# Row sums of an attention kernel: two accumulators, one addition per unit, and a moved row-sum matmul

## The chip, the cores and the metric

The kernel runs on 1 core of one Trainium2 chip. The core has a matrix engine (TensorE, PE in the profile, with PEld for its weight loads), a vector engine (VectorE, DVE), a scalar engine (ScalarE, ACT), GpSimd (POOL) and SyncE (SP), whose queue issues nearly all DMAs here. The metric is the device time of one execution in microseconds.

## The reference

Four layers in turn on x of 2048 x 1024: attention, spectral filter, attention, spectral filter, each with a layer norm ahead and a residual behind. Only the attention's core is touched by the timing questions here.

```python
def _A_ref(x, wqkv, wo):            # B, S, D = 1, 2048, 1024; H = 32 heads of 32
    qkv = (x @ wqkv).reshape(B, S, 3, H, Dh).transpose(2, 0, 3, 1, 4)
    q, k, v = qkv[0], qkv[1], qkv[2]
    scores = jnp.einsum("bhqd,bhkd->bhqk", q, k) * (Dh ** -0.5)
    p = _softmax(scores, axis=-1)
    o = jnp.einsum("bhqk,bhkd->bhqd", p, v)
    return o.transpose(0, 2, 1, 3).reshape(B, S, D) @ wo

def _B_ref(x, w_r, w_i):
    X = rfft2(x) * (w_r + 1j * w_i)
    return irfft2(X, s=(S, D))

x = x + _A_ref(_layernorm(x), A_wqkv, A_wo)
x = x + _B_ref(_layernorm(x), B_w_r, B_w_i)
# and both once more, with the same weights
```

## The kernel before

The softmax is computed without a maximum per row: a bound per group of heads, from norms of q and k, is subtracted (`norms`, `mkbias`), the exponentials are summed, and the product with V is divided by the sum at the end.

**Stages of a layer.** A prologue (`ln`, L300 to L324) normalises 16 tiles of 128 rows, splits each into a high and a low float16 half (`split`, L165: ScalarE makes the high half at L167, VectorE the low half at L168) and transposes both by DMA (L322, on the SP queue). Beside it the first projections run. Then comes the chunk loop, then the end of the output projection with the folding for the spectral stage, then `spectral`.

**The chunk loop** (from L626) runs over 8 groups of 4 heads, in each over 4 chunks `c` of 512 queries, and in each over 16 units `kt` of 128 keys, so a layer has 512 units and 32 chunks. A unit does this:

- `S` (L552): 12 matmuls give the scores of 4 heads into two PSUM tiles of 128 x 2 x 512 (L558), and ScalarE takes the exponential of each into a tile `p` of 128 x 1024 (L562). The pool `psS` has 3 such PSUM tiles, and `pp` has 8 tiles `p`, that is 4 units.
- `PV` (L564): every second unit, the products with V for the two units before it (L568).
- `add` (L575): VectorE adds the unit's two tiles `p` to the two accumulators `acc[0]` and `acc[1]`, 128 x 1024 each (L581). Unit 0 has no addition; unit 1 writes `p0 + p1` into the accumulator (L579).
- a fill in odd units: 8 to 24 matmuls of the next groups' projections (`qk_chunk`, L340; `v_tiles`, L384), or of the output projection in the last two groups (`wo_part`, `wo_rest`, L443). `qk_chunk` collects a sum in the one PSUM bank of `psX`, which is free again when L167 and L168 have read it.

`fin` (L583) ends a chunk: four matmuls with a matrix of ones sum the accumulators over the partitions (L587, into a tile of `psS`), VectorE transposes (L588), takes the reciprocal (L590), transposes back (L593) and scales the output (L594). `out` (L597) splits it to float16 at unit 5 of the next chunk (L600 on ScalarE, L601 on GpSimd) and stores it.

`add` of a unit is written two units later. So the last unit of a chunk is added in the text of unit 1 of the next chunk, and `fin` stands right behind it, after the scores of unit 1 and ahead of that unit's fill.

**What sets the order.** In the chunk loop TensorE and ScalarE run in the order in which the program writes their instructions (`manual_schedule`). The order on VectorE, GpSimd and SP, and everywhere outside the loop but for TensorE at the end of the attention, is chosen by a planner that places an instruction when it expects its inputs. Each engine then works through its queue in order. Slots of a pool are waited for tile by tile: a tile's slot is free when all that used the tile is done.

**Where the accumulators lie.** A buffer `R` of 128 x 16384 floats holds x, K, Q, V and, in its last 2048 columns, the two accumulators (L204, L205). The profile calls all of them `R`.

`pp` serves other stages too: the normalised tile and its two halves (`xn` and `hl`, L316 to L318), residual tiles (`xres`), folding tiles (L512), and tiles `tt` and `sd` in `spectral` (L966, L984).

Of the kernel before, what the change touches and what calls it, by code (L numbers as in the profile page):

```python
# [188 lines left out]
class AttnPools:  # L189


    def __init__(self, tc):
        self.tc = tc
        self.low = Pools(tc, "left")
        self.big = self.low("at_x", 1).tile([128, 16384], F32, name="big")
        self.right = Pools(tc, "right")
        r = self.right("at_r", 1).tile([128, 16384], F32, name="R")
        self.x = r.rearrange("p (t d) -> p t d", d=1024)
        k = r.bitcast(F16).rearrange("p (t a n) -> p t a n", a=2, n=2048)
        self.k = [k[:, i] for i in (3, 4, 5)]  # L200
        self.q = k[:, 2]
        v = r.rearrange("p (a t c) -> p a t c", t=16, c=128)
        self.v = [v[:, i] for i in (0, 1, 6)]
        a = r.rearrange("p (a j n) -> p a j n", j=2, n=512)  # L204
        self.acc = [a[:, i] for i in (14, 15)]  # L205

    def close(self):
        self.small.close()
        self.right.close()
        self.low.close()  # L210

    def open_small(self):
        small = self.small = Pools(self.tc, "left")
        self.pp = small("at_p", 8)
        self.qp = small("at_q", 1)
        self.oc = small("at_oc", 1)
        self.sgp = small("at_stage", 3)
        self.wqp = small("at_wqk", 2)
        self.wvp = small("at_wv", 1)
        self.sq = small("at_sq", 1)  # L220
        self.on = small("at_on", 2)
        self.on2 = small("at_on2", 2)
        self.sm = small("at_sm", 2)
        self.stages = [(self.sgp, "wst")] * 3 + [(self.on, "zt")] * 2 + [(self.on2, "ohl")] * 2
# [45 lines left out]
def attention(nc, tc, layer, ap, xin, yd, wts, wo, cst, dram, flags):  # L270
# [3 lines left out]

    W, prep = wts.W, wts.prep
    od = dram.tile([2, NG, 128, 2048], F16, name=f"od{layer}")
    small, psum = ap.small, Pools(tc, None)
# [22 lines left out]
    def ln(t0, n):  # L300
# [13 lines left out]
        for i in range(n):  # L314
            t = t0 + i
            xn = pp.tile([128, 1024], F32, name="xn", tag="p")  # L316
            nc.scalar.activation(xn, ap.x[:, t], AF.Identity, bias=b[:, i:i + 1], scale=r[:, i:i + 1])
            hl = pp.tile([128, 2, 1024], F16, name="hl", tag="p")  # L318
            split(nc, hl[:, 0], hl[:, 1], xn, SX)
# [126 lines left out]
    def xres(c, t):  # L446
        if c == 3:
            x = pp.tile([128, 1024], F32, name="xres", tag="p")
        else:
# [58 lines left out]
    def fold_rests():  # L508

        r, b = scale_bias(mvs, 12, 1.0)  # L510
        for t in SPILL + [t for t in range(12) if t not in SPILL]:
            f = pp.tile([128, 1024], F32, name="xn", tag="p")  # L512
            nc.scalar.activation(f, wo_dst[t], AF.Identity, bias=b[:, t:t + 1], scale=r[:, t:t + 1])
# [35 lines left out]

    P, O, acc = {}, {}, ap.acc  # L550

    def S(g, c, kt):  # L552

        s = [psS.tile([128, 2, 512], F32, name="s") for _ in range(2)]
        for i, (a, b) in enumerate(((0, 0), (0, 1), (1, 0))):
            for h in range(4):
                r = slice(32 * h, 32 * h + 32)
                nc.tensor.matmul(s[h // 2][:, h % 2], K[g][r, a, kt * 128:kt * 128 + 128],  # L558
                                 Q[g][r, b, c * 512:c * 512 + 512], start=i == 0, stop=i == 2)
        for hf in range(2):  # L560
            p = P[g, c, kt, hf] = pp.tile([128, 2, 512], F32, name="p")
            nc.scalar.activation(p, s[hf], AF.Exp, bias=bias[g], scale=SCALE / (SQ * SQ))  # L562

    def PV(g, c, kt):  # L564
        if kt == 0:
            O[g, c] = psO.tile([128, 512], F32, name="o")
        for h in range(4):
            nc.tensor.matmul(O[g, c][32 * h:32 * h + 32], V[g][:, kt, 32 * h:32 * h + 32], P[g, c, kt, h // 2][:, h % 2],  # L568
                             start=kt == 0, stop=kt == NKT - 1)
# [5 lines left out]
    def add(g, c, kt):  # L575
        for hf in range(2):
            p = P[g, c, kt, hf]
            if kt == 1:
                nc.vector.scalar_tensor_tensor(acc[hf], P[g, c, 0, hf], 1e-34, p, op0=ALU.add, op1=ALU.add)  # L579
            elif kt:  # L580
                nc.vector.tensor_add(acc[hf], acc[hf], p)  # L581

    def fin(g, c):  # L583
        zt = on.tile([128, 16, 32], F32, name="zt")
        z = psS.tile([128, 2, 512], F32, name="s")[:, 0]
        for h in range(4):
            nc.tensor.matmul(z[32 * h:32 * h + 32], cst["ones"], acc[h // 2][:, h % 2], start=True, stop=True)  # L587
        nc.vector.transpose(zt.rearrange("p a b -> p (a b)"), z)  # L588
# [17 lines left out]

    pend, done, late = [], [], []
    fill, lwo, wof = filler(), load_wo(), wo_parts()
# [16 lines left out]
    with tc.manual_schedule(engines={mybir.EngineType.PE, mybir.EngineType.Activation}):  # L625
        for g in range(NG):  # L626
# [3 lines left out]
            for u in range(NCH * NKT):  # L630
                c, kt = divmod(u, NKT)
                S(g, c, kt)
                if kt % 2 == 0:
                    for w in pend:
                        PV(*w)
                    late = pend
                    pend = []
                for w in late[:1]:
                    add(*w)
                    if w[2] == NKT - 1:  # L640
                        fin(*w[:2])
                        done = [w[:2]]
                late = late[1:]
# [106 lines left out]
def spectral(nc, tc, ap, yd, xout, a, cst, fast, flags=None, nxt=None):  # L750
# [209 lines left out]
    nc.sync.dma_start(mi, a["mm" + sfx][:, 2:4])  # L960

    def t2(i, g):
        pt = ps.tile([128, 4, 128], F32, name="ps")
        for j in range(4):
            nc.tensor.transpose(pt[:, j], bufA[:, g, :, 4 * i + j], ident)
        tt = ap.pp.tile([128, 4, 128], F32, name="tt", tag="p")  # L966
        nc.scalar.copy(tt, pt)
        return tt

    sd = {}  # L970

    def ai(i, tt):
# [9 lines left out]
        if i < 14:  # L982
            if i % 2 == 0:
                sd[0] = ap.pp.tile([128, 8, 128], F32, name="sd", tag="p")  # L984
            e = ap.on.tile([128, 4, 128], F32, name="e", tag="zt")
# [251 lines left out]
```

## Time and profile before

| | |
|---|---|
| median of 3 runs | 3907.49 us (3906.37 to 3912.81) |
| profiled execution, span from first to last instruction | 3906.3 us; the page gives no time outside it |
| mean granted TensorE clock | 0.986 |
| chunk loop, layer 0 / layer 1 | from about 126 to 1660 us / 2081 to 3600 us |
| exponentials L562 | 2048 of 1.11 us |
| additions L581, L579 | 1792 and 128 |
| row-sum matmuls L587 | 64 groups of 4, recorded as 8 each |

A page gives the busy time of each engine and its share of the span, then groups of instructions in the form "line engine operation out<-in xcount | busy us, mean ns of one | idle us before them <-what ended it". Rows of the timeline give start, duration, engine, line, operation and count, and in brackets the idle time of the engine just before and what ended it. Rows of the chain give start, duration and what ran. SPq is the SP queue's own issue time. A view by line also lists who waited for that line, with microseconds and times. Matmul ends are modelled, and a float32 matmul shows as two records.

### The profile page before, as it was taken

The numbers are of one execution on the slowest core, as the hardware profiler recorded it, in microseconds if no ns is written. First come the engines' busy times: TensorE is split into PE (matmuls) and PEld (weight loads), VectorE is DVE, ScalarE is ACT, GpSimd is POOL, SyncE is SP. The second block draws the span as 40 slices with busy tenths as digits, with TensorE's granted clock in tenths as the row PEclk, the third lists the DMA queues.
The fourth block names the chain that finished last, engine by engine and source line by source line (L and its number), as shares of the span: only waits on it lengthen the run. The fifth ranks groups of instructions, "written<-read, shape, count | busy, mean of one in ns | idle before, by whom it ended". The sixth has DMA issues, their size and how long they took to land.

```text
span 3906.3 us, 79627 instructions
## 1 busy us (share of the span) xinstructions
PE 3737.0 (96%) x32951; PEld 1642.5 (42%) x32951; DVE 3181.5 (81%) x3793; ACT 2899.6 (74%) x3567; POOL 637.5 (16%) x560
## 2 busy tenths in 40 slices
PE   6999999999999999989989999999999999999998
PEld 4322432342234233368853334333423432333788
DVE  6689899889998987966665998889899888788554
ACT  4577787888788865657855888888888887666686
POOL 1111011101110200014321221122121102000143
PEclk9999999999999999999999999999999999999999
DMA  8000000000000221134170000000000002111333
GB/s 203 15 12 23 12 12 17 18 12 17 15 23 7 71 71 64 64 139 142 62 176 12 15 23 12 12 18 22 10 18 12 23 12 90 52 68 66 146 97 105
DMA packets 165573, 194.07 MB, mean 50 GB/s; under 512 B 74960, under 2 KB 120656, under 8 KB 164176
## 3 DMA queue, kind: packets, MB, share of 16 engines
q1 hardware_dynamic: 164912, 188.82, 15.2%
q8 instruction: 260, 4.26, 0.4%
q14 instruction: 113, 0.93, 0.1%
q10 hardware_dynamic: 288, 0.07, 0.0%
HBM read 123.83 MB, written 48.23 MB: 44 GB/s over the span
## 4 chain that ended last, share of the span: by engine, by line
PE 75%; DVE 10%; issue 7%; ACT 4%; DMA 2%; POOL 2%; SPq 0%; DVEq 0%; ACTq 0%; POOLq 0%
PE o L568 21%; PE s L558 17%; PE x L340 13%; PE x L384 7%; PE x L443 6%; ACT p L562 2%; DVE R L581 2%; PE ps L862 2%; PE ps L800 1%; PE s L587 1%; DMA w<-in_w 1%; PE ps L791 1%; PE s L443 1%; PE ps L977 1%; PE o L384 1%
## 5 line engine op out<-in xcount | busy, mean ns | idle before, releaser
L562 ACT ACTIVATE p<-s,bias 128x1024 f32<-128x1024 f32 x2048 | 2169.0, 1111 | 589.9 <-PE s L558 578.4
L581 DVE TENSOR_TENSOR R<-R,p 128x1024 f32<-128x1024 f32 x1792 | 2146.8, 1251 | 148.3 <-ACT p L562 144.2
L568 PE MATMUL o<-p,R 128*32 128x512 f32 x8192 | 986.1, 599 | 0.0
L340 PE MATMUL x<-big,wqk 128*128 128x512 f16 x2880 | 685.6, 384 | 21.9 <-DVE R L168 8.1
L558 PEld LDWEIGHTS <-R 32*128 32x128 f16 x12288 | 232.5, 92 | 780.2 <-issue 664.6
L340 PEld LDWEIGHTS <-wqk 128*128 128x128 f16 x3072 | 277.9, 98 | 460.1 <-issue 167.5
L558 PE MATMUL s<-R 32*128 32x512 f16 x6144 | 432.5, 379 | 19.1 <-ACT p L562 15.6
L558 PE MATMUL s<-Q,R 32*128 32x512 f16 x6144 | 433.0, 378 | 11.9 <-ACT p L562 10.6
L568 PEld LDWEIGHTS o<-p,R 128*32 128x32 f32 x8192 | 213.9, 109 | 525.6 <-issue 525.0
L601 POOL TENSOR_TENSOR ohl<-zt,ohl 128x512 f16<-128x512 f32 x62 | 180.3, 2907 | 1473.6 <-ACT ohl L600 1473.6
L384 PEld LDWEIGHTS <-big 128*128 128x128 f16 x3072 | 295.0, 99 | 159.7 <-issue 79.1
L384 PE MATMUL x<-wv,big 128*128 128x256 f16 x2688 | 323.2, 277 | 40.6 <-DMA big<-hl 34.6
L579 DVE SCALAR_TENSOR_TENSOR R<-p 128x1024 f32<-128x1024 f32 x128 | 153.9, 1204 | 198.7 <-ACT p L562 198.4
L344 POOL TENSOR_TENSOR sq<-R 128x512 bf16<-128x512 f16 x96 | 144.5, 1505 | 693.8 <-ACT R L167 690.6
L443 PE MATMUL x<-big 128*128 128x512 f16 x1050 | 237.4, 380 | 0.0
L443 PEld LDWEIGHTS <-big 128*128 128x128 f16 x1344 | 126.3, 98 | 177.3 <-issue 33.9
L910 DVE TENSOR_TENSOR H<-G,H 128x512 f16<-128x512 f32 (+1 forms) x68 | 46.9, 690 | 104.7 <-ACT H L909 104.6
L862 PE MATMUL ps<-cbi,H 128*128 128x256 f16 (+1 forms) x792 | 99.2, 273 | 5.6 <-ACT H L909 3.3
L855 ACT COPY U<-ps 64x256 f32<-64x256 f32 (+1 forms) x272 | 97.0, 357 | 8.5 <-PE ps L862 3.3
L855 ACT COPY B<-ps 64x256 f32<-64x256 f32 (+1 forms) x272 | 97.0, 356 | 6.7 <-PE ps L862 3.2
L344 POOL TENSOR_TENSOR sq<-Q 128x512 bf16<-128x512 f16 x32 | 44.6, 1395 | 319.7 <-ACT Q L167 319.7
L862 PE MATMUL ps<-cb,big 128*128 128x256 f16 x780 | 96.4, 273 | 0.0
(429 smaller groups left out, 3017.1 us busy)
## 6 DMA issues: line engine op xcount, KB each, us to landing
wst<-in_wp SPq DMA_DIRECT2D x96, 256.0 KB, 3.0
R<-y SPq DMA_DIRECT2D x32, 512.0 KB, 5.4
w<-in_w SPq DMA_DIRECT2D x60, 256.0 KB, 2.6
od<-ohl SPq DMA_DIRECT2D x56, 256.0 KB, 2.4
big<-od SPq DMA_DIRECT2D x16, 896.0 KB, 6.6
y<-R SPq DMA_DIRECT2D x20, 512.0 KB, 2.7
R<-in_x SPq DMA_DIRECT2D x16, 512.0 KB, 5.6
wst<-in_wo SPq DMA_DIRECT2D x32, 256.0 KB, 2.9
```

What stands on the lines that cost most here:

```text
L340: nc.tensor.matmul(ps, a, b, start=d == 0 and i == 0, stop=d == 7 and i == 2)
L344: nc.gpsimd.tensor_tensor(nrm[ph][:, c], t[:, 0], t[:, 0], op=ALU.mult)
L384: nc.tensor.matmul(ps[:, j], l, r, start=d == 0 and i == 0, stop=d == 7 and i == 2)
L443: nc.tensor.matmul(p, a, b, start=start and d == ds[0] and i == 0, stop=stop and d == ds[-1] and i == 2)
L558: nc.tensor.matmul(s[h // 2][:, h % 2], K[g][r, a, kt * 128:kt * 128 + 128], Q[g][r, b, c * 512:c * 512 + 512], start=i == 0, stop=i == 2)
L562: nc.scalar.activation(p, s[hf], AF.Exp, bias=bias[g], scale=SCALE / (SQ * SQ))
L568: nc.tensor.matmul(O[g, c][32 * h:32 * h + 32], V[g][:, kt, 32 * h:32 * h + 32], P[g, c, kt, h // 2][:, h % 2], start=kt == 0, stop=kt == ...
L579: nc.vector.scalar_tensor_tensor(acc[hf], P[g, c, 0, hf], 1e-34, p, op0=ALU.add, op1=ALU.add)
L581: nc.vector.tensor_add(acc[hf], acc[hf], p)
L601: eng.tensor_tensor(t[:, 1], r, t[:, 0], op=ALU.subtract)
L855: nc.scalar.copy(ov[64 * r:64 * r + 64, a0:a0 + m, x], tl[64 * x:64 * x + 64, :m, r])
L862: nc.tensor.matmul(out, l, r, start=k == 0, stop=k == len(mm_) - 1)
```

## The change

There are six edits.

1. `acc` becomes two accumulators of 128 x 2048: the old place in `R`, and a new pool `at_acc` of 8 KB per partition. Chunks use them in turn (`acc[c % 2]`).
2. The two exponentials of a unit go into the halves of one tile `p` of 128 x 4 x 512. `pp` has 4 tiles of double size instead of 8, and one addition of 128 x 2048 replaces two of 128 x 1024.
3. `fin` is called at unit 2 of the next chunk, right after `PV` of its units 0 and 1, and no longer at unit 1. `out` stays at unit 5.
4. `xn` and `hl` of the prologue share one double tile.
5. Residual and folding tiles and `sd` are halves of a double tile, handed out in turn by a new function `half`; the `tt` tiles of two steps share one.
6. The scratch for dynamic DMAs is set to 4096 bytes per partition.

```diff
-        a = r.rearrange("p (a j n) -> p a j n", j=2, n=512)
-        self.acc = [a[:, i] for i in (14, 15)]
+        self.acc0 = r[:, 14336:16384]
...
+    def half(self, name):
+
+        if self.halves % 2 == 0:
+            self.pair = self.pp.tile([128, 2, 1024], F32, name=name, tag="p")
+        self.halves += 1
+        return self.pair[:, (self.halves - 1) % 2]
+
     def open_small(self):
+        self.halves = 0
         small = self.small = Pools(self.tc, "left")
-        self.pp = small("at_p", 8)
+        self.pp = small("at_p", 4)
+        self.accp = small("at_acc", 1)
...
-            xn = pp.tile([128, 1024], F32, name="xn", tag="p")
+            pair = pp.tile([128, 2, 1024], F32, name="xn", tag="p")
+            xn, hl = pair[:, 0], pair[:, 1].bitcast(F16).rearrange("p (a n) -> p a n", a=2)
             nc.scalar.activation(xn, ap.x[:, t], AF.Identity, bias=b[:, i:i + 1], scale=r[:, i:i + 1])
-            hl = pp.tile([128, 2, 1024], F16, name="hl", tag="p")
...
-            x = pp.tile([128, 1024], F32, name="xres", tag="p")
+            x = ap.half("xres")
...
-            f = pp.tile([128, 1024], F32, name="xn", tag="p")
+            f = ap.half("xn")
...
-    P, O, acc = {}, {}, ap.acc
+    P, O, acc = {}, {}, [ap.acc0, ap.accp.tile([128, 2048], F32, name="acc")]
...
+        p = P[g, c, kt] = pp.tile([128, 4, 512], F32, name="p")
         for hf in range(2):
-            p = P[g, c, kt, hf] = pp.tile([128, 2, 512], F32, name="p")
-            nc.scalar.activation(p, s[hf], AF.Exp, bias=bias[g], scale=SCALE / (SQ * SQ))
+            nc.scalar.activation(p[:, 2 * hf:2 * hf + 2], s[hf], AF.Exp, bias=bias[g], scale=SCALE / (SQ * SQ))
...
     def add(g, c, kt):
-        for hf in range(2):
-            p = P[g, c, kt, hf]
-            if kt == 1:
-                nc.vector.scalar_tensor_tensor(acc[hf], P[g, c, 0, hf], 1e-34, p, op0=ALU.add, op1=ALU.add)
-            elif kt:
-                nc.vector.tensor_add(acc[hf], acc[hf], p)
+        t, p, q = acc[c % 2], *(P[g, c, k].rearrange("p h n -> p (h n)") for k in (kt, 0))
+        if kt == 1:
+            nc.vector.scalar_tensor_tensor(t, q, 1e-34, p, op0=ALU.add, op1=ALU.add)
+        elif kt:
+            nc.vector.tensor_add(t, t, p)
...
-            nc.tensor.matmul(z[32 * h:32 * h + 32], cst["ones"], acc[h // 2][:, h % 2], start=True, stop=True)
+            nc.tensor.matmul(z[32 * h:32 * h + 32], cst["ones"], acc[c % 2][:, 512 * h:512 * h + 512], start=True, stop=True)
...
                     late = pend
                     pend = []
+                    if kt == 2 and full:
+                        done = [full.pop()]
+                        fin(*done[0])
                 for w in late[:1]:
                     add(*w)
                     if w[2] == NKT - 1:
-                        fin(*w[:2])
-                        done = [w[:2]]
+                        full = [w[:2]]
...
-        tt = ap.pp.tile([128, 4, 128], F32, name="tt", tag="p")
+        if i % 2 == 0 and g == 0:
+            sd["tt"] = ap.pp.tile([128, 4, 4, 128], F32, name="tt", tag="p")
+        tt = sd["tt"][:, i % 2 * 2 + g]
...
-                sd[0] = ap.pp.tile([128, 8, 128], F32, name="sd", tag="p")
+                sd[0] = ap.half("sd").rearrange("p (q t) -> p q t", q=8)
...
-    nc = _bacc.Bacc("TRN2", target_bir_lowering=False, num_devices=1)
+    nc = _bacc.Bacc("TRN2", target_bir_lowering=False, num_devices=1, dynamic_dma_scratch_size=4096)
```

More of the change, by code (lines that the diff above doesn't have):

```diff
@@ L275, in attention @@
     W, prep = wts.W, wts.prep
+    ap.halves = 0
     od = dram.tile([2, NG, 128, 2048], F16, name=f"od{layer}")
@@ L567, in PV @@
         for h in range(4):
-            nc.tensor.matmul(O[g, c][32 * h:32 * h + 32], V[g][:, kt, 32 * h:32 * h + 32], P[g, c, kt, h // 2][:, h % 2],
+            nc.tensor.matmul(O[g, c][32 * h:32 * h + 32], V[g][:, kt, 32 * h:32 * h + 32], P[g, c, kt][:, h],
                              start=kt == 0, stop=kt == NKT - 1)
@@ L605, in out @@
             olast[c] = t
-    pend, done, late = [], [], []
+    pend, done, late, full = [], [], [], []
     fill, lwo, wof = filler(), load_wo(), wo_parts()
@@ L960, in spectral @@
     nc.sync.dma_start(mi, a["mm" + sfx][:, 2:4])
+    sd = {}
     def t2(i, g):
@@ L965, in t2 @@
             nc.tensor.transpose(pt[:, j], bufA[:, g, :, 4 * i + j], ident)
-        tt = ap.pp.tile([128, 4, 128], F32, name="tt", tag="p")
+        if i % 2 == 0 and g == 0:
+            sd["tt"] = ap.pp.tile([128, 4, 4, 128], F32, name="tt", tag="p")
+        tt = sd["tt"][:, i % 2 * 2 + g]
         nc.scalar.copy(tt, pt)
         return tt
-    sd = {}
     def ai(i, tt):
```

## The prediction

> **What bounds the kernel now.** I read the page first (busy shares), then the groups of instructions and the windows, then the timeline around chunk boundaries.
>
> ```profile
> span 3906.3 us, 79627 instructions
> PE 3737.0 (96%) x32951; PEld 1642.5 (42%) x32951; DVE 3181.5 (81%) x3793; ACT 2899.6 (74%) x3567; POOL 637.5 (16%) x560
> L562 ACT ACTIVATE p<-s,bias 128x1024 f32<-128x1024 f32 x2048 | 2169.0, 1111 | 589.9 <-PE s L558 578.4
> L581 DVE TENSOR_TENSOR R<-R,p 128x1024 f32<-128x1024 f32 x1792 | 2146.8, 1251 | 148.3 <-ACT p L562 144.2
> L579 DVE SCALAR_TENSOR_TENSOR R<-p 128x1024 f32<-128x1024 f32 x128 | 153.9, 1204 | 198.7 <-ACT p L562 198.4 <-PE s L587 0.3
> ```
>
> TensorE is busy 96% of the span. ScalarE's exponentials (L562) idle 590 us, nearly all of it until TensorE's scores are there, and VectorE's additions (L581, L579) idle 343 us until the exponentials are there. So TensorE leads, ScalarE follows, VectorE comes last. The windows say where TensorE still idles (columns: window, its length, then PE, PEld, DVE busy):
>
> ```profile
> 600.00:660.00 60.00, 57.92 (x514) 17.81 (x511) 54.76 (x56) 48.01 (x51) 11.12 (x10) 1.00 0.06 19
> 2520.00:2580.00 60.00, 60.00 (x541) 18.34 (x540) 54.86 (x54) 48.82 (x51) 14.06 (x6) 1.00 0.04 14
> ```
>
> In layer 0 (first row) 2.08 us of 60 are idle, in layer 1 nothing, with VectorE equally busy. So quicker additions win only where TensorE waits for VectorE. There are two such places: the bank of the next projection, freed by VectorE's half of the split (L168; its view lists who waited), and the row-sum matmul (L587).
>
> ```profile
>   PE x L340: 15.6, 13
>   PE x L384: 6.0, 3
> 364.09 1.84 PE L587 MATMUL s<-R,ones 128*32 128x512 f32 x8
> 731.82 2.10 PE L587 MATMUL s<-R,ones 128*32 128x512 f32 x8 [0.59 <-DVE R L581]
> 914.77 2.09 PE L587 MATMUL s<-R,ones 128*32 128x512 f32 x8 [0.49 <-DVE R L581]
> 1007.72 1.06 PE L587 MATMUL s<-R,ones 128*32 128x512 f32 x8
> ```
>
> The row sum takes 1.06 us when the sums are ready; in 6 of 64 chunks, all in layer 0, it takes 1.84 to 2.10. L168 costs 15.6 + 6.0 = 21.6 us in 16 waits.
>
> **The change, part by part.**
>
> *Two additions become one.*
>
> ```profile
> 1008.98 1.23 DVE L579 SCALAR_TENSOR_TENSOR R<-p 128x1024 f32<-128x1024 f32 x1 [2.85 <-ACT p L562]
> 2229.03 9.21 DVE L581 TENSOR_TENSOR R<-R,p 128x1024 f32<-128x1024 f32 x8
> L588 DVE STREAM_TRANSPOSE zt<-s 128x512 f32<-128x512 f32 x64 | 45.4, 709 | 0.0
> L594 DVE SCALAR_TENSOR_TENSOR zt<-oc,zt 128x512 f32<-128x512 f32 x64 | 44.2, 690 | 1.9
> 2095.08 1.83 PE x L340 x8
> 2096.92 0.76 PE s L558 x12
> 2097.68 1.85 PE o L568 x16
> 253.13 0.83 PE L558 MATMUL s<-R 32*128 32x512 f16 x12
> 257.42 0.68 DVE L168 SCALAR_TENSOR_TENSOR Q<-x,Q 128x512 f16<-128x512 f32 x1
> ```
>
> 512 columns take 0.69 us and 1024 take 1.23, so 512 more cost 0.54 and 2048 should take 2.31 us alone. Eight in a row take 9.21 us: 1.23 for the last, 1.14 apart before it, so 2.28 a unit. An overlap of the same 0.09 makes the new one 2.22 in a row: 0.06 saved a unit, 58 us of VectorE over 64 x 15 units, beside TensorE's path.
>
> A lone unit ends later, though. Today the first half is added during the second exponential, and the pair ends about 1.25 us after it; the whole addition can only start there and ends 2.31 after it, 1.06 late. Waiting for that are the row sum (moved, below) and L168, which VectorE runs behind the addition of its unit. In the quiet case L168 today ends 4.2 us after its unit's scores (253.13 + 0.76 to 257.42 + 0.68); after the shortest fill TensorE wants the bank at 1.83 + 0.76 + 1.85 + 0.76 = 5.2. The shift uses up this margin and passes it by 0.06. Under a backlog the exponential doesn't set the start, and only the saved 0.06 counts. I take 0 for the quiet case (bounds 0 and 112 evacuations x 0.06 = 7 us). For the backlog:
>
> ```profile
> 608.59 7.74 DVE L581 TENSOR_TENSOR R<-R,p 128x1024 f32<-128x1024 f32 x6
> 616.25 0.68 DVE L168 SCALAR_TENSOR_TENSOR Q<-x,Q 128x512 f16<-128x512 f32 x1
> 616.98 2.75 PE L340 MATMUL x<-big,wqk 128*128 128x512 f16 x12 [2.08 <-DVE Q L168]
> ```
>
> Three units of additions stand before this L168, so it comes 0.2 us earlier. Nine such waits of about 2 us: **-1.8 us** (bounds 0, and -21.6 if all L168 waits went).
>
> [...]
>
> *The row sum moves behind the next chunk's first product with V.* Its 1.06 us stay. Its waits go: six times 0.8 to 1.0 us, 5.6 together, and the idle 0.59 and 0.49: **-6.7 us** (0 if VectorE then binds these chunks at L168). What is late next is its PSUM slot. The scores have three slots, taken in turn, and the row sum holds one until the transpose L588 has read it. Behind the product, the scores of unit 4 want that slot: 0.76 (scores of unit 3) + 1.83 (fill) = 2.6 us after the row sum. VectorE starts the addition of unit 2 some 2 x 1.11 + 0.2 us after that unit's scores, which is 1.85 + 1.06 - 2.42 = 0.49 before the row sum ends; the transpose behind it ends 2.31 - 0.49 + 0.71 = 2.53 after. It fits by 0.07 us. I take **+2 us** in all; bounds 0 (transpose first) and 56 boundaries x 2.2 (one addition more ahead of it) = 123; far nearer to 0, since in the row order above the transpose stands directly behind one addition. VectorE's other small row-sum steps (0.7 + 0.7 + 0.4 us) now fall among additions and no longer into the idle 2.85 us (row 1008.98), which the 0.06 x 14 saved units half repay; 0.
>
> In the last group an output-projection tile runs at unit 3 of chunks 2 and 3 and needs that slot at once:
>
> ```profile
> 1557.06 0.81 PE s L558 x12
> 1557.75 1.47 PE L443 MATMUL s<-big,ohl 128*128 128x512 f16 x6
> 1560.03 0.82 PE s L558 x10
> ```
>
> Its six matmuls would start 2.53 - 0.76 = 1.8 us later. The next scores wait until 1560.03 for the exponentials already, so only about 0.9 is left over. Four places: **+3.6 us** (0 to 7).
>
> *Two accumulators.* They remove no wait by themselves: L579, which overwrites the sums, waits 198 us for L562 and 0.3 for L587.
>
> *Pairs of tiles.* In the normalisation a hi/lo tile now shares its slot with its source, so L317 of tile t waits until the transposing DMAs of t-4 have landed; today sources and hi/lo tiles recycle separately.
>
> ```profile
> 2018.39 3.29 SPq L322 DMA_TRANSPOSE big<-hl  x2
> 2023.30 3.10 SPq L322 DMA_TRANSPOSE big<-hl  x2
> 2019.87 1.24 ACT L317 ACTIVATE xn<-R,lb,r 128x1024 f32<-128x1024 f32 x1 [0.60 <-DMA big<-hl]
> 2024.73 1.24 ACT L317 ACTIVATE xn<-R,lb,r 128x1024 f32<-128x1024 f32 x1 [2.53 <-DMA big<-hl]
> 2026.56 3.61 PE L340 MATMUL x<-big,wqk 128*128 128x512 f16 x16 [0.86 <-ACT R L388]
> 68.81 3.34 DMA wst<-in_wp
> ```
>
> Counting the SP queue's issues, these two L317 (tiles 14, 15) wait for tiles 9 and 10; afterwards for 10 and 11, one step of the queue later (2023.30 - 2018.39 = 4.9 us). The evacuation L388 is queued behind tile 15 on ScalarE, TensorE already waits for it, and its work is unbroken from there: **+4.8 us** in layer 1 (0 if L388 is put first, 8 if the L167 before it slips too). In layer 0 the slip is about 2 us beside a weight load on the path (68.81): **+1** (0 to 2). The SP queue issues the same transposes in the same order with tiles waiting for it, and loses nothing.
>
> *The rest.* Half tiles for the residual and the folding and quads in the spectral stage hold as many bytes in flight as now: 0, behind unbroken matmuls (without that cover one 1.2 us folding step a layer). The smaller DMA scratch: no row shows a use of it, 0. The extra 8 KB moves what lies behind it, and the weight loads at the end of layer 0 with it: 0, bounds -3 and +3, one DMA like the 3.34 us above.
>
> **Sum**, against the profiled 3906.3 us (the page shows no time outside the span; the median of the runs is 1.2 above it): -1.8 - 6.7 + 2 + 3.6 + 4.8 + 1 = +2.9 us. On the median of 3907.5 that is 3910 us.
>
> **The rivals.**
>
> *Faster: VectorE was the hidden bound of layer 0.* If its waits vanish, the gain is 21.6 + 6.7 us and 3.2 for two fills that ran slowly after a wait (12 matmuls take 2.75 at 616.98):
>
> ```profile
> 246.15 4.44 PE L340 MATMUL x<-big,wqk 128*128 128x512 f16 x12 [2.08 <-DVE Q L168]
> 307.10 4.27 PE L340 MATMUL x<-big,wqk 128*128 128x512 f16 x12 [2.38 <-DVE R L168]
> ```
>
> Half of these 31 us without the losses gives 3892 us, all of them 3876. For it: VectorE is busy 55 of 60 us. Against: 0.06 us a unit is small beside waits of 2 us.
>
> *Slower: the row sum's slot.* With one more VectorE job before the transpose, such as an L168 (0.68 us), the scores of unit 4 wait 0.6 us or more. It decides from the point where the transpose ends over 2.6 us after the row sum. On 56 boundaries: +34 with the other terms, about 3944 us. For it: a margin of 0.07. Against: chunks with longer fills (2.75) have 0.9 us more room.
>
> *Slower: L168 behind the longer addition.* If VectorE also runs 0.25 us late at the 112 evacuations, the margin is passed by 0.3 each: +34 too, 3944. For it: no margin is left. Against: today's margin of 1.0 us is passed in 16 places only.
>
> [...]
>
> *Slower: GpSimd starved.*
>
> ```profile
> 2323.78 9.17 DVE L581 TENSOR_TENSOR R<-R,p 128x1024 f32<-128x1024 f32 x8
> 2325.90 8.07 POOL L601 TENSOR_TENSOR ohl<-zt,ohl 128x512 f16<-128x512 f32 x1 [9.16 <-ACT ohl L600]
> 2336.00 0.58 PE L357 MATMUL s<-sq,bones 128*32 128x512 bf16 x1 [2.16 <-POOL sq L344]
> ```
>
> While additions run without a gap, GpSimd's L601 took 8.07 us and the norms on TensorE waited 2.16. If longer additions make that the rule at the 28 norms of the chunk loop, +60: 3970. Against: one row of this kind needed eight additions in a row.
>
> *It does nothing measurable*: that is the forecast.
>
> **How the numbers follow.** A measurement of this kernel tells 0.2%, 7.8 us, from no change. Forecast, inside that: 0.36 (3900 to 3915). Faster: 0.27. Slower: slot 0.17, L168 0.11, GpSimd 0.04, prologue and last group at their upper bounds without the gain (2 + 8 + 7 + 2, about 3926) 0.05; together 0.37. The range 3885 to 3950 takes in more than half of the gain and either wait at 0.6 or 0.3 us.
>
> **What would show it.** Right: L581 x896 near 2.3 us; no L587 over 1.1; L168 waits still near 20 us; the last L317 of layer 1 waiting longer for DMA; TensorE busy about 3737. Wrong: score matmuls L558 with idle time ended by L588 (slot), L168 waits doubled, or gone (faster), or more L357 waits ended by L344.

## The result, and the profile after

The changed kernel takes 3971.4 us (median of its runs, 3968.8 to 3974.6) against 3910.1 us for the kernel before in the same runs: a ratio of 1.0155, 95% interval 1.0142 to 1.0167, so about 61 us slower. The forecast was 3910 us with a range up to 3950, and the time lies above it. The first fence is from the page of the changed kernel: span, busy shares, then groups of instructions (busy time, mean of one, idle time before them and what ended it). Lines are numbered anew: L558, L562, L568 are now L567, L571, L577; the additions L581 and L579 are L589 and L587; the row sum L587 is L595 and its transpose L588 is L596; L340, L384 and L443 are L349, L393 and L452.

```profile
span 3972.8 us, 76727 instructions
PE 3739.7 (94%) x32951; PEld 1654.6 (42%) x32951; DVE 3146.4 (79%) x2833; ACT 2897.7 (73%) x3567; POOL 698.2 (18%) x560
L571 ACT ACTIVATE p<-s,bias 128x1024 f32<-128x1024 f32 x2048 | 2169.9, 1112 | 699.6 <-PE s L567 692.0
L589 DVE TENSOR_TENSOR R<-R,p 128x2048 f32<-128x2048 f32 x448 | 1055.6, 2356 | 141.0 <-ACT p L571 125.7
L589 DVE TENSOR_TENSOR acc<-acc,p 128x2048 f32<-128x2048 f32 x448 | 1058.8, 2363 | 122.2 <-ACT p L571 110.2
```

TensorE's busy time is 3739.7 us, 2.7 more than before; all the rest of the 66.5 us between the two profiled spans is idle time of TensorE. VectorE is busy 35 us less than before, and still TensorE now waits for it. Its list of waits (us in total, times, longest) names the places:

```profile
PE x L349 <- DVE R L168: 44.8, 28, 3.0
PE x L349 <- DVE Q L168: 21.5, 8, 4.1
PE x L393 <- DVE R L168: 19.7, 7, 4.8
PE s L567 <- DVE mqk L368: 8.0, 13, 1.0
PE s L452 <- DVE zt L596: 6.8, 4, 1.7
PE s L567 <- DVE zt L596: 6.3, 16, 0.7
```

The waits of the projections for L168, VectorE's half of the split, were 8.1 + 6.2 + 6.0 = 20.3 us in 14 waits in this view of the kernel before; now they are 86.0 us in 43. The two kinds of wait for zt are the row sum's PSUM slot: 13.1 us, which were not there before. The windows of the two chunk loops say where it happens. They go from a layer's first score matmul to its last; two score matmuls that the changed kernel runs ahead of the loop, at 61 us, are left out. The columns are length, busy time of PE, PEld, DVE, ACT and POOL, then the granted clock, the DMA share and GB/s. First the kernel before:

```profile
125.75:1651.24 1525.49, 1486.50 (x13583) 511.10 (x13583) 1350.31 (x1376) 1181.68 (x1246) 170.15 (x115) 0.99 0.08 28
2080.38:3588.64 1508.26, 1480.07 (x13583) 510.08 (x13583) 1322.75 (x1302) 1181.78 (x1246) 225.56 (x115) 0.99 0.08 28
```

and the changed one:

```profile
125.67:1684.33 1558.66, 1486.32 (x13583) 517.38 (x13583) 1329.85 (x898) 1181.43 (x1246) 228.71 (x115) 0.99 0.08 27
2119.57:3659.93 1540.36, 1480.24 (x13583) 515.56 (x13583) 1309.19 (x824) 1181.32 (x1246) 228.21 (x115) 0.99 0.08 27
```

The loops are 33.2 and 32.1 us longer with the same matmul time: 65.3 of the 66.5 us. Layer 1, whose loop lost 1.5 us to L168 in these three kinds before, now loses 37.3 (layer 0: 18.8, now 48.2). Between the loops the kernel is 6.1 us longer, and after the last scores 4.8 us shorter; why that last stretch is shorter wasn't followed up (in the runs below it takes 313 to 318 us).

One chunk head of layer 1 shows how. Timeline of the kernel before, VectorE and ScalarE's L167 (start, duration; brackets: idle before, and what ended it; the small steps between are left out):

```profile
2452.49 1.23 DVE L579 SCALAR_TENSOR_TENSOR R<-p 128x1024 f32<-128x1024 f32 x1 [3.74 <-ACT p L562]
2453.63 0.71 DVE L588 STREAM_TRANSPOSE zt<-s 128x512 f32<-128x512 f32 x1
2456.47 0.69 DVE L594 SCALAR_TENSOR_TENSOR zt<-oc,zt 128x512 f32<-128x512 f32 x1
2457.09 9.23 DVE L581 TENSOR_TENSOR R<-R,p 128x1024 f32<-128x1024 f32 x8
2465.32 0.61 ACT L167 ACTIVATE R<-x 128x512 f16<-128x512 f32 x1
2466.23 0.69 DVE L168 SCALAR_TENSOR_TENSOR R<-x,R 128x512 f16<-128x512 f32 x1
```

and the same place in the changed kernel:

```profile
2501.02 2.29 DVE L587 SCALAR_TENSOR_TENSOR R<-p 128x2048 f32<-128x2048 f32 x1 [3.81 <-ACT p L571]
2503.61 2.29 DVE L589 TENSOR_TENSOR R<-R,p 128x2048 f32<-128x2048 f32 x1 [0.30 <-ACT p L571]
2505.82 0.71 DVE L596 STREAM_TRANSPOSE zt<-s 128x512 f32<-128x512 f32 x1
2507.69 0.69 DVE L602 SCALAR_TENSOR_TENSOR zt<-oc,zt 128x512 f32<-128x512 f32 x1
2508.30 7.93 DVE L589 TENSOR_TENSOR R<-R,p 128x2048 f32<-128x2048 f32 x3
2512.72 0.61 ACT L167 ACTIVATE R<-x 128x512 f16<-128x512 f32 x1
2516.15 0.68 DVE L168 SCALAR_TENSOR_TENSOR R<-x,R 128x512 f16<-128x512 f32 x1
2516.88 1.89 PE L349 MATMUL x<-big,wqk 128*128 128x512 f16 x8 [1.57 <-DVE R L168]
```

Before, L168 starts 0.30 us after L167 ends (2465.93); now it starts 2.82 us after (2513.33). All but 0.10 of the 2.52 us of lateness are three things. VectorE starts the chunk's first addition 13.44 us ahead of L167's end before and 12.31 now, because it waits for the second exponential: 1.13. It waits once more, 0.30, for unit 2. And three units of additions up to L168 take 7.85 us, where four took 9.14 before, that is 6.86 for three: 0.99.

### The profile page after: what moved, and what is told of

Same layout as the page of the kernel before. It is cut to its first block, busy times and chain, and to the rows that moved or that the text cites. A ratio compares the mean times of both kernels' runs of the same rounds, so it can differ in the third digit from the quotient of the medians.

```text
span 3972.8 us, 76727 instructions
## 1 busy us (share of the span) xinstructions
PE 3739.7 (94%) x32951; PEld 1654.6 (42%) x32951; DVE 3146.4 (79%) x2833; ACT 2897.7 (73%) x3567; POOL 698.2 (18%) x560
## 4 chain that ended last, share of the span: by engine, by line
PE 64%; DVE 23%; ACT 4%; DMA 4%; issue 4%; POOL 1%; SPq 0%; DVEq 0%; POOLq 0%; ACTq 0%
PE o L577 17%; PE s L567 14%; PE x L349 10%; DVE acc L589 8%; PE x L393 7%; DVE R L589 6%; PE x L452 6%; ACT p L571 3%; PE ps L872 2%; PE ps L810 2%; DMA wst<-in_wp 1%; PE s L452 1%; PE ps L801 1%; PE ps L989 1%; DVE acc L587 1%
## 5 line engine op out<-in xcount | busy, mean ns | idle before, releaser
L571 ACT ACTIVATE p<-s,bias 128x1024 f32<-128x1024 f32 x2048 | 2169.9, 1112 | 699.6 <-PE s L567 692.0
L589 DVE TENSOR_TENSOR R<-R,p 128x2048 f32<-128x2048 f32 x448 | 1055.6, 2356 | 141.0 <-ACT p L571 125.7
L589 DVE TENSOR_TENSOR acc<-acc,p 128x2048 f32<-128x2048 f32 x448 | 1058.8, 2363 | 122.2 <-ACT p L571 110.2
L577 PE MATMUL o<-p,R 128*32 128x512 f32 x8192 | 985.1, 598 | 0.0
L349 PE MATMUL x<-big,wqk 128*128 128x512 f16 x2880 | 696.3, 388 | 75.5 <-DVE R L168 44.8
L567 PEld LDWEIGHTS <-R 32*128 32x128 f16 x12288 | 234.3, 92 | 790.0 <-issue 674.9
L349 PEld LDWEIGHTS <-wqk 128*128 128x128 f16 x3072 | 282.3, 99 | 506.6 <-issue 217.9
L567 PE MATMUL s<-R 32*128 32x512 f16 x6144 | 435.9, 379 | 20.5 <-ACT p L571 9.9
L567 PE MATMUL s<-Q,R 32*128 32x512 f16 x6144 | 431.9, 378 | 12.6 <-ACT p L571 8.7
L577 PEld LDWEIGHTS o<-p,R 128*32 128x32 f32 x8192 | 213.7, 109 | 524.7 <-issue 524.1
L393 PE MATMUL x<-wv,big 128*128 128x256 f16 x2688 | 326.8, 279 | 56.3 <-DMA big<-xn 36.6
L609 POOL TENSOR_TENSOR ohl<-zt,ohl 128x512 f16<-128x512 f32 x62 | 123.3, 1989 | 1433.2 <-ACT ohl L608 1433.2
L393 PEld LDWEIGHTS <-big 128*128 128x128 f16 x3072 | 296.5, 100 | 157.7 <-issue 75.3
L353 POOL TENSOR_TENSOR sq<-R 128x512 bf16<-128x512 f16 x96 | 212.6, 2214 | 697.1 <-ACT R L167 696.8
L452 PE MATMUL x<-big 128*128 128x512 f16 x1050 | 237.4, 380 | 0.0
L452 PEld LDWEIGHTS <-big 128*128 128x128 f16 x1344 | 126.2, 98 | 172.0 <-issue 28.4
L587 DVE SCALAR_TENSOR_TENSOR R<-p 128x2048 f32<-128x2048 f32 x32 | 73.4, 2292 | 123.0 <-ACT p L571 123.0
L353 POOL TENSOR_TENSOR sq<-Q 128x512 bf16<-128x512 f16 x32 | 69.0, 2156 | 359.1 <-ACT Q L167 339.8
L587 DVE SCALAR_TENSOR_TENSOR acc<-p 128x2048 f32<-128x2048 f32 x32 | 73.3, 2291 | 65.4 <-ACT p L571 65.4
```

What stands on the lines that cost most here:

```text
L349: nc.tensor.matmul(ps, a, b, start=d == 0 and i == 0, stop=d == 7 and i == 2)
L353: nc.gpsimd.tensor_tensor(nrm[ph][:, c], t[:, 0], t[:, 0], op=ALU.mult)
L393: nc.tensor.matmul(ps[:, j], l, r, start=d == 0 and i == 0, stop=d == 7 and i == 2)
L452: nc.tensor.matmul(p, a, b, start=start and d == ds[0] and i == 0, stop=stop and d == ds[-1] and i == 2)
L571: nc.scalar.activation(p[:, 2 * hf:2 * hf + 2], s[hf], AF.Exp, bias=bias[g], scale=SCALE / (SQ * SQ))
L587: nc.vector.scalar_tensor_tensor(t, q, 1e-34, p, op0=ALU.add, op1=ALU.add)
```

## The experiments

Three theories stood at first: that the joined addition's late start at the head of a chunk is carried to L168 (START), that a joined addition loses more time beside GpSimd (PORT), and that the moved row sum puts VectorE's small steps in the way (MOVE). Lengths of the loops, in us, are from each run's profile, from a layer's first score matmul to its last. A ratio compares with the kernel before on the same chip. Loops and spans are each of one execution, on several chips, between which the median of the kernel before varies from 3905.6 to 3912.1 us:

| kernel | ratio to before (95%) | loop 0 | loop 1 | span |
|---|---|---|---|---|
| before | 1 | 1525.5 | 1508.3 | 3906.3 |
| changed | 1.0155 (1.0142 to 1.0167) | 1558.7 | 1540.4 | 3972.8 |
| e1 all additions in halves | 1.0027 (1.0018 to 1.0037) | 1537.2 | 1511.7 | 3920.2 |
| e2 row sum at its old place | 1.0081 (1.0061 to 1.0100) | 1547.0 | 1518.5 | 3939.4 |
| e3 both undone | 1.0005 (0.9995 to 1.0014) | 1530.8 | 1508.6 | 3911.9 |
| e4 unit 1 in halves | 1.0127 (1.0108 to 1.0146) | 1557.2 | 1529.2 | 3960.2 |
| e5 units 1 to 3 in halves | 1.0093 (1.0076 to 1.0110) | 1554.0 | 1513.2 | 3939.8 |
| e6 changed, no GpSimd in loop | 1.0070 (1.0054 to 1.0087) | 1540.5 | 1521.7 | 3934.9 |
| e9 before, no GpSimd in loop | 0.9916 (0.9900 to 0.9933) | 1514.2 | 1502.2 | 3882.9 |
| e10 e5 and e6 together | 1.0047 (1.0030 to 1.0064) | 1548.8 | 1507.0 | 3927.7 |
| e12 changed, no maxima in loop | 1.0120 (1.0084 to 1.0157) | 1534.2 | 1536.2 | 3943.0 |
| e13 e5, no maxima in loop | 0.9974 (0.9964 to 0.9983) | 1515.8 | 1513.1 | 3898.3 |
| e14 before, no maxima in loop | 0.9926 (0.9909 to 0.9942) | 1507.4 | 1506.8 | 3877.0 |
| e15 changed, two chains | 1.0131 (1.0114 to 1.0148) | 1556.4 | 1530.7 | 3958.1 |
| e16 e2, two chains | 1.0028 (1.0019 to 1.0038) | 1536.4 | 1506.7 | 3916.8 |

One of e12's four runs, 3973.9 us, pulls its ratio up; the other three take 3945.0 to 3949.2 us.

**Which part of the change costs it: e1 to e4.** e1 writes every addition in halves:

```diff
-        if kt == 1:
-            nc.vector.scalar_tensor_tensor(t, q, 1e-34, p, op0=ALU.add, op1=ALU.add)
-        elif kt:
-            nc.vector.tensor_add(t, t, p)
+        for hf in range(2):
+            sl = slice(1024 * hf, 1024 * hf + 1024)
+            if kt == 1:
+                nc.vector.scalar_tensor_tensor(t[:, sl], q[:, sl], 1e-34, p[:, sl], op0=ALU.add, op1=ALU.add)
+            elif kt:
+                nc.vector.tensor_add(t[:, sl], t[:, sl], p[:, sl])
```

> The changed kernel with each addition of 128x2048 written as two of 128x1024; the moved row sum, the two accumulators and the tile pairs stay. The changed kernel takes 3971 us, the one before 3910. Theory START (the joined addition can begin only after the second exponential; at the head of a chunk, where VectorE has nothing else to do, that is 1.1 us later, and the lateness is carried through the additions without a gap to L168): most of the 63 us of L168 waits go, about 3925 us, with some 13 us of waits for the row sum's transpose left. Theory PORT (an addition of 2.3 us loses more time to GpSimd than two of 1.2): also about 3925. Theory MOVE (the row sum's small VectorE steps, 2.5 us, now stand among additions): no gain from this, 3955 us or more.

e2 puts the row sum back:

```diff
-                    if kt == 2 and full:
-                        done = [full.pop()]
-                        fin(*done[0])
...
-                        full = [w[:2]]
+                        fin(*w[:2])
+                        done = [w[:2]]
```

> The changed kernel with the row sum back at unit 1, behind its scores; the joined addition, the two accumulators and the tile pairs stay. MOVE: the L168 waits fall back, about 3920 us. START and PORT: the L168 waits stay, only the 13 us of waits for the row sum's transpose go and the waits of the row sum for the last, now longer addition come back and grow (64 chunks x up to 1 us): 3955 to 3985 us.

e3 is both edits:

> The changed kernel with both undone: additions of 128x1024 and the row sum at unit 1. Left of the change are the two accumulators, the pairs of tiles and the smaller DMA scratch. All theories: 3912 to 3917 us, that is the kernel before plus the 5 us of the second prologue. If it is above 3930, the pairs of tiles or the place of things in SBUF cost what I put down to additions and row sums.

and e4 is the edit of e1 for the addition of unit 1 (L587) alone:

```diff
         if kt == 1:
-            nc.vector.scalar_tensor_tensor(t, q, 1e-34, p, op0=ALU.add, op1=ALU.add)
+            for hf in range(2):
+                sl = slice(1024 * hf, 1024 * hf + 1024)
+                nc.vector.scalar_tensor_tensor(t[:, sl], q[:, sl], 1e-34, p[:, sl], op0=ALU.add, op1=ALU.add)
```

> The changed kernel with only the first addition of each chunk (unit 1, L587) written as two of 128x1024, 64 of 960; all else stays. START: VectorE begins a chunk 1.1 us earlier, and at least half of the 63 us of L168 waits goes: 3930 to 3945 us. PORT: 14 of 15 additions of a chunk are as long as before, so at most 5 us are gained: 3966 us or more. MOVE: the same, 3966 or more.

Measured: 3922.1, 3941.4, 3912.8 and 3963.0 us, beside 3909.2 for the kernel before on that chip. e3 leaves 3.6 us: accumulators, pairs of tiles and DMA scratch are not the cause. From there joining alone costs 28.6 us (e2), moving alone 9.3 (e1), and both 58.6 (the changed kernel's 3971.4): 21 us more than their sum. So neither START nor MOVE is right by itself. In e2 two places pay: TensorE waits 43.2 us for L168 in the three kinds, and at its old place the row sum waits 14.3 us for the joined additions (1.1 before). e4 is a miss for START: the first addition in halves wins 8 us, not 25 or more. Its trace says why: VectorE starts earlier and then waits longer for unit 2's second exponential, 1.23 us where the changed kernel waited 0.30.

```profile
2491.95 2.36 DVE L589 SCALAR_TENSOR_TENSOR R<-p 128x1024 f32<-128x1024 f32 x2 [2.80 <-ACT p L571]
2495.55 2.29 DVE L591 TENSOR_TENSOR R<-R,p 128x2048 f32<-128x2048 f32 x1 [1.23 <-ACT p L571]
```

**How far the head of the chunk reaches: e5 and e6.** e5 halves the additions of units 1 to 3:

```diff
+        for hf in range(2 if kt < 4 else 1):
+            n = 1024 if kt < 4 else 2048
+            sl = slice(n * hf, n * hf + n)
```

e6 takes two operations of the loop from GpSimd to ScalarE:

```diff
-        nc.gpsimd.tensor_tensor(nrm[ph][:, c], t[:, 0], t[:, 0], op=ALU.mult)
+        nc.scalar.activation(nrm[ph][:, c], t[:, 0], AF.Square)
...
-        eng.tensor_tensor(t[:, 1], r, t[:, 0], op=ALU.subtract)
+        nc.scalar.copy(t[:, 1], r)
```

> The changed kernel with the additions of units 1, 2 and 3 of each chunk in two halves of 128x1024, the other 12 joined. All in halves gave 3922 us, only unit 1 gave 3963. Theory FLOOR (wherever VectorE has caught up with ScalarE, a joined addition ends 2.3 us after the second exponential and a pair 1.25; at the head of a chunk it has caught up in units 1 and 2, and only what it is late there reaches L168): most of the gain of all halves, 3925 to 3940 us. Theory PORT (every joined addition loses time when GpSimd runs beside it): 3 of 15 additions, at most a quarter of the 41 us still open, 3950 us or more.

> The changed kernel with GpSimd's two operations of the chunk loop taken to ScalarE: the squares for the norms (L353), and in place of the subtraction that makes the low half of the output (L609) a plain copy, so that the low half is not the difference any more. PORT: the additions that now take 2.66 us a unit beside GpSimd take 2.25, VectorE wins some 40 us a layer, and the L168 waits fall to about half: 3940 us or less. FLOOR: the additions get shorter too, but the lateness from the head of the chunk stays, 3955 us or more.

Measured: 3942.4 and 3934.8 us, beside 3905.6 before. e5 lies just above the upper end of FLOOR's forecast, and the two layers differ: in layer 1 halving 3 of 15 additions takes back 27 of 32 us, in layer 0 only 5 of 33. In layer 1 the place shown above reads, in e5:

```profile
2499.80 2.29 DVE L592 TENSOR_TENSOR R<-R,p 128x2048 f32<-128x2048 f32 x1 [0.23 <-ACT p L571]
2500.17 0.61 ACT L167 ACTIVATE R<-x 128x512 f16<-128x512 f32 x1
2502.01 0.68 DVE L168 SCALAR_TENSOR_TENSOR R<-x,R 128x512 f16<-128x512 f32 x1
2502.75 1.89 PE L349 MATMUL x<-big,wqk 128*128 128x512 f16 x8
```

VectorE has caught up by unit 5 (it waits 0.23 us for ScalarE again), L168 starts 1.23 us after L167's end, and TensorE doesn't wait. Halves at the head of the chunk start earlier and, as shown below, also follow one another faster (2.28 us a unit against 2.39); e5 doesn't separate the two.

e6 answers PORT's forecast too, so it needed its control, e9: the same edit in the kernel before.

> The control to the run of the changed kernel without GpSimd in the loop (3935 us): the kernel before with the same two operations taken to ScalarE (squares; a plain copy in place of the subtraction for the low half of the output, which so is not the difference any more). If GpSimd costs the joined additions more than the halves, the change costs less without it: 3895 to 3905 us, a gap of 30 to 40 us in place of 62. If it costs both the same, the gap stays: 3870 to 3882 us.

e9 takes 3880.7 us. Without GpSimd's two operations the change still costs 1.0070 / 0.9916 = 1.0155 by the ratios, as much as with them, and 52 us by the profiled spans (3934.9 - 3882.9) instead of 66.5. Both kernels are faster without them (ratios of 1.0070 for 1.0155, and 0.9916), and PORT falls as the main cause. How much it adds stays open: by the ratios nothing, give or take 9 us, while in the loops of the two profiles, which are from different chips, the gap narrows from 65.3 to 45.8 us. At the place shown above it counts: the third of the three additions ahead of L168 runs beside two operations of GpSimd and lasts 3.14 us instead of 2.29, which is 0.85 of the 0.99 us found there.

```profile
2513.08 3.14 DVE L589 TENSOR_TENSOR R<-R,p 128x2048 f32<-128x2048 f32 x1
2512.90 1.18 POOL L609 TENSOR_TENSOR ohl<-zt,ohl 128x512 f16<-128x512 f32 x1 [42.48 <-ACT ohl L608]
2514.03 3.10 POOL L353 TENSOR_TENSOR sq<-R 128x512 bf16<-128x512 f16 x1
```

**The other layer: e10 and e12 to e14.** e10 joins e5 and e6:

> The changed kernel with the additions of units 1 to 3 in halves (alone 3942 us, -29) and without GpSimd's two operations in the loop (alone 3935 us, -36; the low half of the output is a plain copy). FLOOR and PORT as two terms that shorten the same lateness: if it is passed on in full, 3906 us; if the one leaves little for the other, 3920 us or more.

It takes 3930.4 us, so the two gains don't add up. In layer 1 nothing but 4.8 us is left against e9, in layer 0 34.6. What layer 0 has besides are the maxima of the weights. Timeline of e5 there:

```profile
610.66 1.28 DVE L168 SCALAR_TENSOR_TENSOR wqk<-wst,wqk 128x512 f16<-128x512 f32 x2
614.65 0.69 DVE L268 TENSOR_REDUCE wm<-wst 128x1 f32<-128x512 f32 x1 [2.71 <-DMA wst<-in_wp]
```

The planner has put the maximum directly behind the split, with no addition between, so that VectorE stands still for a weight load: 30.7 us before L268 in all, where the changed kernel has 18.5. e12 to e14 take these maxima out, in the changed kernel, in e5 and in the kernel before. The expectation counts 36 pairs of operations; it is 40 (48 less the 8 of the first weights).

```diff
-            if self.flag is not None:
+            if self.flag is not None and ph in PH0:
```

> The changed kernel without the maxima of the weights that layer 0's chunk loop forms for a range flag (36 pairs of operations on VectorE that the loop's weights need; those of the first weights stay). One cause: layer 0's loop, 1559 us, falls to layer 1's 1540, in all about 3953 us.

> The changed kernel with the additions of units 1 to 3 in halves, and without the maxima of the weights in layer 0's chunk loop. One cause (the head of the chunk, as in layer 1): layer 0's loop falls from 1554 to about 1513 us, in all about 3899 us. If joined additions cost layer 0 in another way: 1530 us or more in layer 0's loop, 3915 us or more.

> The control: the kernel before without those maxima in layer 0's chunk loop. Its layer 0 should behave as its layer 1 (1508 us), about 3890 us, and the change should cost in it what it costs in layer 1, about 32 us a layer.

Measured: 3947.2, 3900.0 and 3879.1 us. Now layer 0 behaves as layer 1 in all three (rows e12 to e14 of the table), and with the three halves 18 of the 27 us in layer 0 come back, beside 23 of 29 in layer 1. So layer 0 needs no second cause; the maxima hid the recovery. Whether by their place in the queue or by their work isn't separated, since these runs take away both. e14 lies 11 us under its forecast; in 8.7 of them it reaches layer 0's loop earlier (at 117.0 for 125.8 us).

**Why a lateness lasts: e15 and e16.** VectorE should catch up quickly, since two units take TensorE 5.2 us, as the prediction worked out, and two additions 4.6. But joined additions in a row don't keep the pace that the prediction took. In the changed kernel, at a place where GpSimd begins an operation only in the third addition (2282.37):

```profile
2277.23 7.08 DVE L589 TENSOR_TENSOR acc<-acc,p 128x2048 f32<-128x2048 f32 x3
```

Three joined additions take 7.08 us, so they stand (7.08 - 2.29) / 2 = 2.39 us apart, 0.10 more than one lasts. Each reads the sum that the one before it wrote. The halves of before go to two accumulators in turn and need 2.28 us a unit. By these numbers VectorE gains 0.4 us on TensorE in two units with joined additions, and 0.6 with halves. e15 and e16 keep joined additions but let odd and even units add into different accumulators:

```diff
-        t, p, q = acc[c % 2], *(P[g, c, k].rearrange("p h n -> p (h n)") for k in (kt, 0))
-        if kt == 1:
+        t = acc[(c + kt + 1) % 2]
+        p, q = (P[g, c, k].rearrange("p h n -> p (h n)") for k in (kt, 0 if kt == 1 else kt))
+        if kt in (1, 2):
```

> The changed kernel with the same 15 joined additions of a chunk, but odd units add into one accumulator and even units into the other (unit 2 starts that sum with an operation that reads its tile alone). The row sum reads the accumulator of the odd units only, so that the even units are left out of it. Additions in a row then stand 2.21 us apart instead of 2.39. Theory CHAIN (the dependency slows VectorE's catching up by 0.18 us a unit, and that is what carries lateness to L168): at least 20 of the 65 us that the two loops lose come back, 3952 us or less. Theory FLOOR alone (the late start at the head of the chunk): under 8 us, 3964 us or more.

> The same with the row sum at its old place, unit 1 (with dependent additions 3941 us; with halves 3913 us). CHAIN: at least 12 of the 28 us between them come back, 3929 us or less. FLOOR alone: 3937 us or more.

In e16 neighbours stand 2.20 us apart (rows below), and it takes 3916.2 us, with 3906.5 before on that chip: of the 26.1 us that joining costs the two loops at the old place of the row sum (e2 against e3), 22.4 come back. At that place breaking the chain gives back nearly the whole cost. The late start is still there; 2.20 us a unit is quicker even than the halves' 2.28, so part of the gain may make up for it.

```profile
2262.59 2.28 DVE L590 TENSOR_TENSOR R<-R,p 128x2048 f32<-128x2048 f32 x1
2264.79 2.28 DVE L590 TENSOR_TENSOR acc<-acc,p 128x2048 f32<-128x2048 f32 x1
2266.99 2.28 DVE L590 TENSOR_TENSOR R<-R,p 128x2048 f32<-128x2048 f32 x1
```

e15, at the new place, takes 3957.6 us (3906.5 before), between the two forecasts. It has a fault of its own: the transpose now stands ahead of unit 2's operation and VectorE waits 65 us in all for the moved row sum. So how chain and late start divide the 59 us where the row sum is moved stays open.

**The order, and two faster kernels: e7, e8, e11.** Each starts from the kernel before. e7 moves only the squares to ScalarE (the first two lines of e6's diff):

> The kernel before, with only the squares for the norms moved from GpSimd to ScalarE. The waits of the norm matmuls for GpSimd (7.5 us in all, 6.5 of them in layer 1) go, and VectorE's additions lose less time beside GpSimd: PORT 3885 to 3898 us, FLOOR about 3900 us.

It takes 3888.4 us, a ratio of 0.9953 (0.9936 to 0.9969), as PORT had it. Its trace shows another chain: GpSimd's subtraction takes 8.71 us (2.91 on average in the kernel before), the store of its result starts on the SP queue at its end (1340.79), a weight load comes late, and the scores wait 6.68 us for ScalarE, which waits 5.95 us for that load. The kernel before has the same chain, and there the order of the queue shows too: the subtraction from 1342.14, 9.31 us beside additions, the store at 1351.48, the weight load's issue right behind it at 1351.95, ScalarE idle for 6.63 us until the load has landed, the scores for 6.70.

```profile
1332.05 8.71 POOL L601 TENSOR_TENSOR ohl<-zt,ohl 128x512 f16<-128x512 f32 x1 [42.52 <-ACT ohl L600]
1340.79 0.38 SPq L603 DMA_DIRECT2D od<-ohl  x1
1344.66 0.63 ACT L167 ACTIVATE big<-wst 128x512 f16<-128x512 f32 x1 [5.95 <-DMA wst<-in_wo]
1346.35 1.46 PE L558 MATMUL s<-R 32*128 32x512 f16 x10 [6.68 <-ACT p L562]
```

e11 therefore also moves that subtraction, to VectorE:

```diff
-    def out(g, c, eng=nc.gpsimd):
+    def out(g, c, eng=nc.vector):
```

> The kernel before with the squares on ScalarE (alone 3888 us) and the subtraction for the low half of the output on VectorE in place of GpSimd. A store of the output then no longer holds the SP queue behind an operation that took 8.7 us of GpSimd: the two waits of 6.7 us of scores for ScalarE go, and VectorE's additions are not slowed. VectorE gets 62 operations of about 0.7 us, 43 us. If that lies in its idle time, 3870 to 3880 us; if it delays the splits L168 or the row sums, 3888 us or more.

It takes 3880.9 us, just above its forecast, a ratio of 0.9918 (0.9901 to 0.9934): with the full computation it is faster than both kernels, 31 us below the one before on its chip. e8 writes VectorE's queue in the order of the text:

```diff
-    with tc.manual_schedule(engines={mybir.EngineType.PE, mybir.EngineType.Activation}):
+    with tc.manual_schedule(engines={mybir.EngineType.PE, mybir.EngineType.Activation, mybir.EngineType.DVE}):
```

> The kernel before, with VectorE's instructions in the chunk loop in the order of the program text and no longer in the planner's. L168 then stands behind fewer additions: if its waits (21.6 us) come from its place in VectorE's queue, they go, about 3890 us. If the text's order puts the row sum's steps and the weights' maxima in front of additions that are ready, VectorE idles more and it is 3915 us or more.

It takes 4030.9 us. The waits for L168 fall as expected (20.3 us to 9.8 in the same three kinds), but the row sum now waits 71.2 us for additions and the scores 34.7 for the norms' maxima. The planner's order is worth more than L168's place.

## Why the prediction was wrong

**The additions.** "2048 should take 2.31 us alone" was right (2.29). "An overlap of the same 0.09 makes the new one 2.22 in a row: 0.06 saved a unit" is the step that failed first. The overlap of 0.09 belonged to additions into different accumulators. In a row the joined one takes 2.39, so it costs 0.11 us a unit against the pairs' 2.28, just where VectorE is late. VectorE's busy time fell by 35 us, not 58, and it did not help, since idle time before the additions grew in its place.

**L168.** "I take 0 for the quiet case" and "Under a backlog the exponential doesn't set the start, and only the saved 0.06 counts" were the second failure: -1.8 us forecast, +65.7 us of waits measured. A backlog has a beginning. At the head of each chunk VectorE has caught up, and there the second exponential does set the start; the 1.1 us lost there is not made up before the next units' L168, since additions in a row are slower than predicted and some run beside GpSimd. How the cost divides among these three is open where the row sum is moved. The rival "L168 behind the longer addition" named this mechanism and its place, but at 0.25 us of lateness (+34 us, chance 0.11). The shown L168 is 2.5 us later than before.

e1 writes the joined additions of VectorE, which is busy 79% of the changed kernel's span and yet holds up TensorE, as two again: 49 us of the 59 come back.

**The row sum.** Its waits went, as forecast: L595 is busy 66.7 us where L587 was 73.8, -7.1 for a forecast of -6.7. The PSUM slot was the right next wait and too small: 6.3 us in 16 waits (forecast +2), and in the last group exactly four, 6.8 us (forecast +3.6, bound 7). "VectorE's other small row-sum steps (0.7 + 0.7 + 0.4 us) now fall among additions and no longer into the idle 2.85 us", a term put at 0, is the third failure: moving costs 9.3 us with additions in halves and 30 with joined ones. That these steps delay additions which can't catch up fits both numbers; no run moves the steps alone.

**The rest.** The prologue of layer 1 was sized well: +4.8 forecast; e3, which keeps the tile pairs, is 4.5 us longer between the loops. Layer 0's prologue cost nothing (+1 forecast). The rival that VectorE is a hidden bound of layer 0 was right that VectorE holds layer 0 back: e14, without the maxima, is 18 us shorter in layer 0's loop and 9 ahead of it. But joined additions did not lighten it. GpSimd was not starved as that rival had it: its subtraction fell from 2.91 to 1.99 us on average, and the norms' waits for its squares from 7.5 to 4.0 us, though the squares themselves got longer (1.51 to 2.21 us).

## What to carry to other kernels

Fewer and longer instructions on an engine that feeds a tighter one can be slower though its busy time falls (here 61 us slower, with VectorE 35 us less busy): ask when the joined one may start, and whether it has to wait for the result of its neighbour, which two smaller ones in turn did not (2.39 us apart against 2.28 for the two). Follow lateness from the last place where the engine had caught up to the first place where another engine waits for it; a mean rate over the span shows neither. Small steps that look free in idle time need not be free elsewhere: moving the row sum, and its steps among the engine's main work, cost 9.3 us here with additions in halves and 30 with joined ones.

## What the runs showed of the hardware

When a 128x2048 addition of VectorE reads what the one before it wrote, it starts 0.10 us after that one's end; neighbours that don't depend on each other overlap by 0.08 (2.39 us apart in the changed kernel, 2.20 in e16). Without GpSimd's two operations in the loop no joined addition lasts over 2.30 us (e6; mean 2.29); with them they go up to 3.21 (mean 2.36), and the halves of before, at most 1.23 without them (e9), up to 2.19. The view by line shows shortest, median and longest in ns, here of the additions into one of the accumulators, first in the changed kernel, then in e6:

```profile
L589 DVE TENSOR_TENSOR acc<-acc,p x448: 2272/2292/3212, 181.8 to 3666.0; 128x2048 f32<-128x2048 f32 x150
L589 DVE TENSOR_TENSOR acc<-acc,p x448: 2272/2292/2294, 181.8 to 3625.5; 128x2048 f32<-128x2048 f32 x150
```

The long additions go with GpSimd's operations: in the trace of the changed kernel all 125 joined additions over 2.30 us run beside one, and the 610 that meet none last 2.29 us on average and at most 2.295; 161 more meet one and are not longer than 2.30. In the kernel before, all 104 halves of L581 over 1.23 us run beside one, and the 1460 that meet none last at most 1.23. Which of two was issued first wasn't followed.
